# The first expert's tokens handled block by block: transposes, splits and products of 128 columns as each gather lands

## The chip, the cores and the metric

The kernel runs on one core of one Trainium2 chip. The metric is the device time of one execution in microseconds (us). Engines are called by the names of the profile: PE is TensorE (PEld its weight loads), DVE is VectorE, ACT is ScalarE, POOL is GpSimd, SP is SyncE, which issues most loads.

## The reference

Three layers stand behind one another on 3072 tokens of 512 numbers: attention with a local window and a few global keys; a mixture of 8 experts, in which each token goes to one expert and each expert takes 384 tokens; and a second feed-forward layer for all tokens. What matters here is the second layer:

```python
logits = x @ w_gate
# greedily by falling logit: each token to one expert, cap = N // E = 384 tokens each
for e in range(E):
    mask = assigned == e
    h = np.maximum(x[mask] @ w1[e], 0.0)      # 512 -> 1024
    out[mask] = h @ w2[e]                     # 1024 -> 512
# then, for all tokens: g = relu(h) + alpha * min(h, 0); g @ w_out  (512 -> 2048 -> 512)
```

## The kernel before, in words

Attention runs first and writes its rows to `x_rows` in DRAM. Then the `Router` finds the experts' token lists one expert after another, and `Experts` computes, for each expert in the order in which they are found, both feed-forward layers on its 384 tokens.

The order of instructions is written out by hand: each engine works through its own queue in the order of the program. The router is a generator, `all_phases`; each `next(gen)` issues one more piece of it between the experts' products. A phase's search is a chain of steps. One `next(gen)` issues the DVE part of a step (lines 552 to 572, then the compare of line 770, the reduce of line 778 and the preparation of line 543); the following one issues the PE product that adds the counts over the partitions (`totals`, line 786), whose result the next DVE part reads.

Numbers of the experts' layers are split in a high and a low part (types fp32r): ACT copies the high part, and another engine subtracts it to get the remainder. A product is then three: high by high, low by high, high by low (`PASSES`). For the weights (`split`, lines 887 to 892) the remainder is made by POOL; for the tokens (`x_split`) and the hidden layer (end of `up1`) by DVE.

The first expert begins as follows. When its number is known, the first tiles of its weights are loaded (`choose`). When its token list is known, `gather` issues three indirect loads on POOL, one for each block of 128 tokens. Until they land, PE computes products of no use (`filler`, line 398), each of up to 512 columns. Then `run` splits the first weight tile (line 1023), issues one DVE part of the second expert's search (line 1024), transposes all three blocks (twelve transposes into four PSUM tiles, one for each quarter of the 512 numbers), splits the four quarters, splits three more weight tiles, and calls `up1(0, 0)`: twelve products of 384 columns, four quarters by three passes. Behind them stands `next(gen)`, the `totals` product of the search, then the loop over all steps: `up1(0, 1)`, `down1(0, 0)`, and so on.

At the end of `up1` the Relu of the result is written twice, by ACT (high part, line 926) and by DVE (remainder, line 927, which waits for ACT's).

Of the kernel before, what the change touches and what calls it, by code (L numbers as in the profile page):

```python
# [9 lines left out]
FT = mybir.dt.float32  # L10
# [5 lines left out]
AF = mybir.ActivationFunctionType  # L16
OP = mybir.AluOpType
# [344 lines left out]
class Router:  # L362
# [35 lines left out]
    def filler(self, columns):  # L398
        nc = self.nc
        ps = self.spare()  # L400
        flat = self.slots.bitcast(BF).rearrange("p s t -> p (s t)")
        while columns > 0:
            n = min(columns, 512)
            nc.tensor.matmul(ps[:, :n], self.ones, flat[:, :n], start=True, stop=True)
            columns -= n
# [193 lines left out]
    def phase(self, k, result):  # L599
        nc, E, TT = self.nc, self.E, self.TT  # L600
# [25 lines left out]
        n = cnt.shape[2]  # L626
# [13 lines left out]
        if k < E - 1:  # L640
# [3 lines left out]
                                op=OP.mult)  # L644
# [15 lines left out]
        ps = self.psum.tile([128, 512], FT, name="r_ps")  # L660
# [19 lines left out]
        for name, op, s in (("r_blk", OP.logical_shift_right, B.bit_length() - 1), ("r_in", OP.bitwise_and, B - 1)):  # L680
            t = w.tile([128, TT], U16, name=name)
# [9 lines left out]
        for c in range(0, TT, chunk):  # L691
# [3 lines left out]
                                    op=OP.is_equal)  # L695
# [4 lines left out]
        ps = self.psum.tile([128, 512], FT, name="r_ps")  # L700
        yield
        for t in range(TT):
            two, one = parts[t // chunk]
            nc.tensor.matmul(ps[:rows, :B], two[:, :, t % chunk], one[:, :, t % chunk], start=(t == 0),  # L704
                             stop=(t == TT - 1))
# [8 lines left out]
        ps = self.psum.tile([128, 512], FT, name="r_ps")  # L714
        nc.tensor.matmul(ps[:, :3], lists.rearrange("p g s -> p (g s)"), self.unit, start=True, stop=True)
        if wide:
            self.filler(5120)
        yield
        idx = w.tile([128, 3], I32, name="r_idx", bufs=8)
        nc.vector.tensor_copy(idx, ps[:, :3])  # L720
# [78 lines left out]
class Experts:  # L799
# [84 lines left out]
        self.nc.sync.dma_start(r, src[:, f, :])  # L884
        self.st["r2", e, f] = r

    def split(self, name, e, f, shape):
        r = self.st.pop(("r" + name, e, f))
        s = self.pair("m_s" + name, shape, 2)
        self.nc.scalar.activation(s[:, 0], r, AF.Copy)  # L890
        self.nc.gpsimd.tensor_tensor(s[:, 1], r, s[:, 0], op=OP.subtract)  # L891
        self.st["s" + name, e, f] = s

    def split_w1(self, e, f):
# [20 lines left out]
    def up1(self, e, f):  # L915
        nc = self.nc
        s1 = self.st.pop(("s1", e, f))
        x = self.ex[e]["x"]
        n = self.NT * 128
        ps = self.hidden.tile([128, 512], FT, name="m_h", bufs=3)  # L920
        for d in range(self.ND):
            for i, (a, b) in enumerate(self.PASSES):
                nc.tensor.matmul(ps[:, :n], s1[:, a, d], x[:, b, d], start=(d == 0 and i == 0),  # L923
                                 stop=(d == self.ND - 1 and i == 2))
        h = self.pair("m_hh", [n], 2)
        nc.scalar.activation(h[:, 0], ps[:, :n], AF.Relu)  # L926
        nc.vector.scalar_tensor_tensor(h[:, 1], ps[:, :n], 0.0, h[:, 0], op0=OP.max, op1=OP.subtract)  # L927
        self.st["h", e, f] = h

    @staticmethod  # L930
    def order(n, last):
# [74 lines left out]
    def run(self, router, n_experts):  # L1006
        nf1, nf2 = self.F1 // 128, self.F2 // 128
        routes = []
        gen = router.all_phases(routes)
        while not (routes and "expert" in routes[0]):  # L1010
            next(gen)
            next(gen)
        self.choose(0, routes[0])
        while "tokens" not in routes[0]:
            next(gen)
            next(gen)
        self.gather(0, routes[0])
        nc = self.nc
        behind = self.consts.tile([1, 1], I32, name="m_behind")
        nc.gpsimd.iota(behind, pattern=[[0, 1]], base=0, channel_multiplier=0)  # L1020
        nc.sync.value_load(behind[0:1, 0:1], min_val=0, max_val=1)
        self.load_rest(0)
        self.split_w1(0, 0)
        next(gen)
        ps = [self.acc.tile([128, 512], FT, name="m_acc", bufs=4) for _ in range(self.ND)]
        for a in range(self.NT):
            for d in range(self.ND):
                self.transpose(ps[d], 0, a, d)
        for d in range(self.ND):
            self.x_split(ps[d], 0, d)  # L1030
        self.split_w1(0, 1)
        self.split_w2(0, 0)
        self.split_w2(0, 1)
        steps = [(e, s, f) for e in range(n_experts) for s, nf in ((1, nf1), (2, nf2)) for f in range(nf)]

        def prepare(e, i):
            if i == 0:
                self.split_w1(e, 0)
            elif i == 1:
                self.split_w2(e, 0)  # L1040
            elif i == 2:
                self.split_w1(e, 1)
            else:
                self.split_w2(e, 1)

        self.up1(0, 0)
        next(gen)
        self.split_w1(0, 2)
        chosen = fetched = 0
        N = len(steps)  # L1050
        for n, (e, s, f) in enumerate(steps):
            if s == 1 and f + 3 < nf1:
                self.load_w1(e, f + 3)
                self.load_w2(e, f + 3)
            full = s == 1 and f == nf1 - 1 or s == 2 and f == 0
            if not full:
                next(gen, None)
            if s == 2 and chosen == e and len(routes) > e + 1 and "expert" in routes[e + 1]:
                chosen = e + 1
                self.choose(e + 1, routes[e + 1])  # L1060
            if s == 2 and fetched == e and len(routes) > e + 1 and "tokens" in routes[e + 1]:
                fetched = e + 1
                self.gather(e + 1, routes[e + 1])
                prepared, ready = 0, n + self.READY
            now = []
            if s == 2 and e + 1 < n_experts and f >= nf2 - 6:
                while fetched > e and n >= ready and prepared < self.ND and len(now) < 1 + (f + self.ND - prepared >= nf2 or f == nf2 - 2):
                    self.x_transpose(e + 1, prepared)
                    now.append(prepared)
                    prepared += 1  # L1070
                assert f < nf2 - 2 or prepared == self.ND
            last = s == 1 and f == nf1 - 1
            ahead = self.AHEAD if e else 2
            if s == 1 and f >= nf1 - ahead:
                self.fetch_wo(e, f - nf1 + ahead)
            if e and s == 2 and f + ahead < nf2:
                self.fetch_wo(e, f + ahead)
            nx = steps[n + 1] if n + 1 < N else None
            if not last and nx:
                (self.up1 if nx[1] == 1 else self.up2)(nx[0], nx[2])  # L1080
                if nx[1] == 1 and nx[2] + 2 < nf1:
                    self.split_w1(nx[0], nx[2] + 2)
            for i in now:
                prepare(e + 1, i)
            (self.down1 if s == 1 else self.down2)(e, f, lambda: full or next(gen, None))
            if last:
                self.up2(e, 0)
            if s == 1 and f + 2 < nf1:
                self.split_w2(e, f + 2)
            if not e and s == 2 and f + 2 < nf2:  # L1090
                self.fetch_wo(e, f + 2)
# [89 lines left out]
```

## Time and profile before

| | |
|---|---|
| median of 3 runs | 1121.75 us (1120.18 to 1121.84) |
| profiled execution | 1119.95 us |
| its span in the trace | 1118.2 us |
| PE busy | 1065.7 us, 95% of the span |
| DVE, POOL, ACT busy | 68%, 48%, 34% |

The profile is that of one execution. The span runs from its first to its last instruction; the profiled execution's own time is 1.75 us longer. Times in the rows are counted from the start of the span. The granted clock of PE is a share of full speed (2.4 GHz).

### The profile page before, as it was taken

How to read it: one execution, taken by the hardware profiler on the slowest of the kernel's cores; microseconds unless marked ns; L12 is line 12 of the kernel's file. 1: busy time of each engine (PE TensorE's matmuls, PEld its weight loads, DVE VectorE, ACT ScalarE, POOL GpSimd, SP SyncE). 2: the span in 40 equal slices, each digit the busy share in tenths (PEclk: the TensorE clock that was granted, in tenths of full speed). 3: DMA queues.
4: the chain of work that ended last, by engine and by line, in shares of the span. 5: the costliest groups of instructions: out<-in, count | busy, mean ns of one | idle time of the engine just before them, and what ended most of it. 6: DMA issues, size and time to landing. Idle time of an engine off the chain costs nothing.

```text
span 1118.2 us, 19406 instructions
## 1 busy us (share of the span) xinstructions
PE 1065.7 (95%) x6659; PEld 944.2 (84%) x6659; DVE 762.9 (68%) x2228; ACT 385.6 (34%) x969; POOL 540.5 (48%) x652
## 2 busy tenths in 40 slices
PE   8989898869999999999999999999999999999997
PEld 6777677648888998899889988898899999999995
DVE  7989888778897878897789698778753323231321
ACT  7777777503322320232133113211331233123211
POOL 4888878315455823462346325432543354236222
PEclk9999999968999999999999999999999999999999
DMA  9788877114135525441534533533353435434131
GB/s 219 212 218 223 209 202 187 49 46 134 57 132 179 173 83 181 130 160 58 198 96 149 163 123 109 157 135 129 95 180 123 133 108 185 131 116 167 57 131 67
DMA packets 151219, 156.55 MB, mean 140 GB/s; under 512 B 83536, under 2 KB 116304, under 8 KB 151120
## 3 DMA queue, kind: packets, MB, share of 16 engines
q1 hardware_dynamic: 147280, 142.72, 42.3%
q0 software_dynamic: 3840, 12.59, 3.4%
q8 instruction: 53, 0.87, 0.3%
q14 instruction: 46, 0.38, 0.1%
HBM read 134.31 MB, written 20.97 MB: 139 GB/s over the span
## 4 chain that ended last, share of the span: by engine, by line
PE 75%; DVE 12%; POOL 6%; issue 3%; ACT 2%; DMA 2%; SPq 0%; DVEq 0%; POOLq 0%; ACTq 0%
PE m_h L963 23%; PE m_acc L988 23%; PE m_h L923 9%; PE m_acc L950 9%; PE a_s L212 2%; PE a_pt L232 2%; PE a_xp L248 2%; DVE r_thr L564 2%; DVE r_red L778 1%; DVE r_cmp L770 1%; PE r_ps L704 1%; POOL wo L82 1%; ACT a_p L221 1%; PE a_cb L277 1%; PE a_tp L169 1%
## 5 line engine op out<-in xcount | busy, mean ns | idle before, releaser
L973 POOL TENSOR_TENSOR m_g<-m_t,m_g 128x384 fp32r<-128x384 f32 (+1 forms) x144 | 140.2, 973 | 372.1 <-ACT m_g L972 369.1
L988 PE MATMUL m_acc<-m_so,m_g 128*128 128x512 f32 x1152 | 298.7, 399 | 0.4 <-POOL m_spacer L996 0.3
L963 PE MATMUL m_h<-m_y,wi 128*128 128x384 f32 x1536 | 294.4, 341 | 0.0
L963 PEld LDWEIGHTS m_h<-m_y,wi 128*128 128x128 f32 x1536 | 273.3, 189 | 7.5
L988 PEld LDWEIGHTS m_acc<-m_so,m_g 128*128 128x128 f32 x1152 | 209.6, 189 | 35.3 <-POOL m_g L973 0.9
L972 ACT ACTIVATE m_g<-m_t 128x384 fp32r<-128x384 f32 (+1 forms) x144 | 70.5, 490 | 435.6 <-DVE m_t L971 255.1
L891 POOL TENSOR_TENSOR m_s<-m_r,m_s 128x512 fp32r<-128x512 f32 x128 | 166.9, 1308 | 103.5 <-ACT m_s L890 103.2
L970 DVE TENSOR_SCALAR m_t<-m_h,m_al 128x384 f32<-128x384 f32 (+1 forms) x144 | 82.2, 571 | 149.2 <-PE m_h L963 136.1
L950 PE MATMUL m_acc<-m_hh,m_s 128*128 128x384 f32 x768 | 150.3, 340 | 1.3 <-DVE m_hh L927 1.3
L923 PE MATMUL m_h<-m_xt,m_s 128*128 128x384 f32 x768 | 146.1, 338 | 0.0
L923 PEld LDWEIGHTS m_h<-m_xt,m_s 128*128 128x128 f32 x768 | 136.4, 190 | 1.9 <-ACT m_xt L872 0.3
L950 PEld LDWEIGHTS m_acc<-m_hh,m_s 128*128 128x128 f32 x768 | 132.4, 188 | 2.9 <-DVE m_hh L927 1.6
L890 ACT ACTIVATE m_s<-m_r 128x512 fp32r<-128x512 f32 x128 | 79.7, 626 | 98.8 <-PE m_acc L950 34.1
L221 ACT ACTIVATE a_p<-a_sx,a_mn 128x232 f32<-128x232 f32 (+1 forms) x192 | 88.5, 462 | 25.8 <-DVE a_mn L218 25.4
L927 DVE SCALAR_TENSOR_TENSOR m_hh<-m_h,m_hh 128x384 fp32r<-128x384 f32 x64 | 35.4, 552 | 76.8 <-ACT m_hh L926 76.2
L971 DVE SCALAR_TENSOR_TENSOR m_t<-m_h,m_t 128x384 f32<-128x384 f32 (+1 forms) x144 | 73.9, 513 | 4.9
L778 DVE TENSOR_REDUCE r_red<-r_cmp 128x24 bf16<-128x576 bf16 (+1 forms) x97 | 73.9, 761 | 3.4
L218 DVE CUSTOM_DVE_ANT_0 a_sx<-a_s,a_bias 128x232 f32<-128x232 f32 (+1 forms) x192 | 61.4, 374 | 11.6 <-PE a_s L212 9.4
L212 PE MATMUL a_s<-a_kz,a_qz 64*128 64x232 f32 (+1 forms) x384 | 50.2, 381 | 18.7 <-POOL a_kz L190 16.2
L926 ACT ACTIVATE m_hh<-m_h 128x384 fp32r<-128x384 f32 x64 | 31.5, 492 | 95.6 <-PE m_h L923 82.3
L770 DVE TENSOR_TENSOR r_cmp<-r_mk,r_thr 128x576 bf16<-128x576 uint16 x78 | 61.4, 787 | 0.0
L212 PEld LDWEIGHTS a_s<-a_kz,a_qz 64*128 64x128 f32 x384 | 33.2, 193 | 28.6 <-POOL a_kz L190 22.6
(183 smaller groups left out, 1283.3 us busy)
## 6 DMA issues: line engine op xcount, KB each, us to landing
m_so<-wo_pairs SPq DMA_DIRECT2D x112, 512.0 KB, 3.3
m_r<-in_moe_w_dram SPq DMA_DIRECT2D x128, 256.0 KB, 3.0
f_raw<-in_moe_w_in_dram SPq DMA_DIRECT2D x16, 512.0 KB, 4.6
f_raw<-in_moe_w_out_dram SPq DMA_DIRECT2D x16, 512.0 KB, 3.7
wo_pairs<-m_so SPq DMA_DIRECT2D x16, 512.0 KB, 2.6
a_k<-in_k_dram SPq DMA_DIRECT2D x24, 256.0 KB, 4.8
a_q<-in_q_dram SPq DMA_DIRECT2D x24, 256.0 KB, 5.2
a_v<-in_v_dram SPq DMA_DIRECT2D x24, 256.0 KB, 4.8
```

What stands on the lines that cost most here:

```text
L212: nc.tensor.matmul(ps[s][:, a, :n], T["Q", g][r, p], kz[r, p, c0:c0 + n], start=True, stop=True)
L221: nc.scalar.activation(pr[:, s, 2 * C - n:], sx[:, s, :n], AF.Exp, bias=T["mn", g][:, h:h + 1], scale=-1.0, accum_out=T["sum", g][:, h:h + 1])
L778: nc.vector.tensor_reduce(red, cmp, axis=AX.X, op=OP.add)
L890: self.nc.scalar.activation(s[:, 0], r, AF.Copy)
L891: self.nc.gpsimd.tensor_tensor(s[:, 1], r, s[:, 0], op=OP.subtract)
L923: nc.tensor.matmul(ps[:, :n], s1[:, a, d], x[:, b, d], start=(d == 0 and i == 0), stop=(d == self.ND - 1 and i == 2))
L950: nc.tensor.matmul(ps[:, :n], s2[:, b, d * 128:(d + 1) * 128], h[:, a], start=(f == 0 and a + b == 0), stop=(last and a == 1))
L963: nc.tensor.matmul(ps[:, :n], self.wi[:, a, d, f * 128:(f + 1) * 128], y[:, b, d], start=(d == 0 and i == 0), stop=(d == self.ND - 1 and i ...
L970: nc.vector.tensor_scalar(t[:, cs], ps[:, cs], 0.0, self.al[:, f:f + 1], op0=OP.min, op1=OP.mult)
L971: nc.vector.scalar_tensor_tensor(t[:, cs], ps[:, cs], 0.0, t[:, cs], op0=OP.max, op1=OP.add)
L973: nc.gpsimd.tensor_tensor(g[:, 1, cs], t[:, cs], g[:, 0, cs], op=OP.subtract)
L988: nc.tensor.matmul(ps, g[:, a, t * 128:(t + 1) * 128], s[:, b], start=(f == 0 and a + b == 0), stop=(last and a == 1))
```

## The change

The tokens of the first expert are handled by blocks. A new function `first_up` transposes a block's four quarters into one PSUM tile, has ACT and DVE split this tile in one instruction each (512 columns), and issues twelve products of 128 columns for it; the order on PE is transposes 0, a filler, transposes 1, products 0, transposes 2, products 1, a filler, products 2. The Relu is issued at the end of `first_up`, before the splits of the next three weight tiles. The remainder of the first weight tile is made by DVE in place of POOL. The `next(gen)` that stood ahead of the transposes now stands behind the splits of the weights, directly ahead of the other one. The filler behind the last product of the token list grows from ten instructions of 512 columns to twelve.

```diff
-            self.filler(5120)
+            self.filler(6144)
...
-    def split(self, name, e, f, shape):
+    def split(self, name, e, f, shape, engine=None):
...
-        self.nc.gpsimd.tensor_tensor(s[:, 1], r, s[:, 0], op=OP.subtract)
+        (engine or self.nc.gpsimd).tensor_tensor(s[:, 1], r, s[:, 0], op=OP.subtract)
...
+        self.relu(ps, e, f)
+
+    def relu(self, ps, e, f):
+        nc, n = self.nc, self.NT * 128
...
+    def first_up(self, filler):
+        nc = self.nc
+        s1 = self.st.pop(("s1", 0, 0))
+        x = self.ex[0]["x"] = self.pair("m_xt", [self.ND, self.NT * 128], 1)
+        out = self.hidden.tile([128, 512], FT, name="m_h", bufs=3)
+
+        def part(a):
+            return slice(a * 128, (a + 1) * 128)
+
+        def turn(a):
+            ps = self.acc.tile([128, 512], FT, name="m_acc", bufs=4)
+            for d in range(self.ND):
+                nc.tensor.transpose(ps[:, part(d)], self.ex[0]["xr"][a][:, part(d)], self.ident)
+            ps = ps.rearrange("p (d t) -> p d t", t=128)
+            hi, lo = x[:, 0, :, part(a)], x[:, 1, :, part(a)]
+            nc.scalar.activation(hi, ps, AF.Copy)
+            nc.vector.tensor_tensor(lo, ps, hi, op=OP.subtract)
+
+        def multiply(a):
+            todo = [(d, i, j) for i, j in self.PASSES for d in range(self.ND)]
+            todo.sort(key=lambda m: m[2])
+            for n, (d, i, j) in enumerate(todo):
+                nc.tensor.matmul(out[:, part(a)], s1[:, i, d], x[:, j, d, part(a)], start=(n == 0),
+                                 stop=(n == len(todo) - 1))
+
+        turn(0)
+        filler(512)
+        turn(1)
+        multiply(0)
+        turn(2)
+        multiply(1)
+        filler(512)
+        multiply(2)
+        self.relu(out, 0, 0)
...
         self.load_rest(0)
-        self.split_w1(0, 0)
-        next(gen)
-        ps = [self.acc.tile([128, 512], FT, name="m_acc", bufs=4) for _ in range(self.ND)]
-        for a in range(self.NT):
-            for d in range(self.ND):
-                self.transpose(ps[d], 0, a, d)
-        for d in range(self.ND):
-            self.x_split(ps[d], 0, d)
+        self.split("1", 0, 0, [self.ND, 128], nc.vector)
+        self.first_up(router.filler)
         self.split_w1(0, 1)
         self.split_w2(0, 0)
         self.split_w2(0, 1)
...
-        self.up1(0, 0)
+        next(gen)
         next(gen)
         self.split_w1(0, 2)
```

## Rows read from the trace of the kernel before

**Rows 1.** The page: busy time, share of the span and instructions.
```profile
PE 1065.7 (95%) x6659; PEld 944.2 (84%) x6659; DVE 762.9 (68%) x2228; ACT 385.6 (34%) x969; POOL 540.5 (48%) x652
```

**Rows 2.** Waits of PE, 250 to 345 us: total us, times, longest.
```profile
PE m_acc L857 <- DMA m_x<-x_rows,r_idx: 2.5, 3, 1.0
PE m_acc L950 <- DVE m_hh L927: 1.3, 1, 1.3
```

**Rows 3.** Stretches: length, busy us of PE, PEld, DVE, ACT, POOL; granted clock; DMA.
```profile
30.00:40.00 10.00, 10.00 (x103) 8.23 (x100) 9.70 (x35) 8.55 (x27) 8.61 (x14) 1.00 0.85 233
...
242.00:246.00 4.00, 3.32 (x31) 1.94 (x29) 2.78 (x16) 0.00 (x0) 0.00 (x0) 0.93 0.23 69
246.00:248.00 2.00, 2.00 (x6) 0.78 (x7) 1.69 (x8) 0.60 (x1) 0.69 (x1) 0.50 0.78 256
...
249.00:250.00 1.00, 1.00 (x5) 0.35 (x3) 0.76 (x2) 0.00 (x0) 0.82 (x1) 0.84 0.69 147
...
252.50:253.50 1.00, 0.95 (x4) 0.56 (x4) 0.96 (x3) 0.00 (x0) 0.00 (x0) 0.62 0.76 234
...
259.00:260.00 1.00, 1.00 (x6) 0.69 (x6) 0.00 (x0) 0.35 (x1) 1.00 (x2) 0.72 0.00 0
```

**Rows 4.** Timeline, 246 to 256 us: start, us, engine, line; idle before, releaser.
```profile
246.07 3.92 PE L404 MATMUL m_h<-r_slots,r_ones 128*128 128x512 bf16 x10
...
250.75 2.03 DVE L770 TENSOR_TENSOR r_cmp<-r_mk,r_thr 128x576 bf16<-128x576 uint16 x1
...
250.91 0.66 PE L857 MATMUL m_acc<-ident,m_x 128*128 128x128 f32 x4 [0.89 <-DMA m_x<-x_rows,r_idx]
...
251.20 1.25 POOL L891 TENSOR_TENSOR m_s<-m_r,m_s 128x512 fp32r<-128x512 f32 x1
...
252.52 0.95 PE L857 MATMUL m_acc<-ident,m_x 128*128 128x128 f32 x4 [0.95 <-DMA m_x<-x_rows,r_idx]
252.81 0.75 DVE L778 TENSOR_REDUCE r_red<-r_cmp 128x24 bf16<-128x576 bf16 x1
...
254.08 1.11 PE L857 MATMUL m_acc<-ident,m_x 128*128 128x128 f32 x4 [0.61 <-DMA m_x<-x_rows,r_idx]
...
255.12 1.95 DVE L873 TENSOR_TENSOR m_xt<-m_acc,m_xt 128x384 fp32r<-128x384 f32 x4 [1.41 <-ACT m_xt L872]
...
255.14 4.48 PE L923 MATMUL m_h<-m_xt,m_s 128*128 128x384 f32 x12
```

**Rows 5.** Timeline, 259 to 264 us.
```profile
259.42 0.24 PE L786 MATMUL r_ps<-r_red,r_ones 128*128 128x24 bf16 x1
...
259.51 2.37 PE L923 MATMUL m_h<-m_xt,m_s 128*128 128x384 f32 x12
259.65 0.49 ACT L926 ACTIVATE m_hh<-m_h 128x384 fp32r<-128x384 f32 x1 [1.87 <-PE r_ps L786]
...
260.74 1.30 POOL L891 TENSOR_TENSOR m_s<-m_r,m_s 128x512 fp32r<-128x512 f32 x1 [0.15 <-ACT m_s L890]
...
261.06 1.07 DVE L564 SCALAR_TENSOR_TENSOR r_thr<-r_dig,r_pre 128x72 uint16<-128x72 f32 x1
...
262.16 0.46 DVE L770 TENSOR_TENSOR r_cmp<-r_mk,r_thr 128x576 bf16<-128x576 uint16 x1
...
262.65 0.75 DVE L778 TENSOR_REDUCE r_red<-r_cmp 128x24 bf16<-128x576 bf16 x1
...
263.46 0.19 PE L786 MATMUL r_ps<-r_red,r_ones 128*128 128x24 bf16 x1
```

**Rows 6.** Timeline, attention, 62 to 64 us.
```profile
62.88 0.66 PE L277 MATMUL a_cb<-a_cmb,a_xt 128*128 128x144 f32 x4
...
63.37 0.60 PE L169 MATMUL a_tp<-ident,a_q 128*128 128x128 f32 x4
```

**Rows 7.** Timeline of DVE, 286 to 300 us.
```profile
287.00 1.43 DVE L770 TENSOR_TENSOR r_cmp<-r_mk,r_step 128x576 bf16<-128x576 uint16 x1
...
299.59 0.23 DVE L564 SCALAR_TENSOR_TENSOR r_thr<-r_dig,r_step 128x72 uint16<-128x72 f32 x1
```

## The prediction

> **What bounds the kernel now.** I read the page first: TensorE (PE) is busy for 95% of the span [rows 1], so the question is where the other 5% lies and whether the change touches it. The waits of PE from 250 us to 345 us answer it [rows 2]: behind the three gathers of the first expert's tokens PE waits 2.5 us, and then in 90 us only 1.3 us more. Whatever delays PE's first expert therefore delays the end by as much; what shortens it shortens the end, unless a wait grows behind it. Third the table by stretches, for the clock [rows 3]: 0.93 at 242 to 246, half speed (1.2 GHz) at 246 to 248 although PE had been 83% busy before; full (2.4 GHz) within 249 to 250, during the fillers; below full again at 252.5 to 253.5, between the gathers; full again only within 259 to 260. Fourth the timeline [rows 4]: blocks of tokens arrive at 250.91, 252.52 and 254.08; the first expert's first twelve products start at 255.14 and end at 259.62, all but the last at half clock. Meanwhile VectorE (DVE) has done a search step for the second expert (its compare at 250.75 held 2.03 us, the reduce behind it). So the product with that step's sums, at 259.42, waits for nothing, and the next twelve products start at 259.51 [rows 5]. That start is my reference point: PE is full from there on.
>
> **The parts that cost nothing.** The remainder of the first weight tile leaves GpSimd (1.25 us at 251.20, [rows 4]) for DVE, right behind the search's first reduce and before the first tokens land; on DVE 512 elements cost about 0.65 us (the remainders of 384 columns, four in 1.95 [rows 4], times 4/3). It was done before the first products needed it, and will be. Three splits of 512 elements in place of four of 384 lie under PE's work on the block before. Two more fillers of 512 columns (3.92/10 = 0.39 us each at most, [rows 4]) fill time before 250.91 in which PE waits for the gather; the filler behind the first transposes lies in the next such wait. The loads queued on SP and the gathers on POOL keep their order; the next weight loads follow GpSimd's remainders, which come later, but for tiles used several steps on.
>
> **The blocks on PE.** Thirty-six products of 128 columns replace twelve of 384. The trace shows no such product in this type. Bounds: below, a third of the 384-column product at full clock, 2.37/12/3 = 0.066 us [rows 5]; above, a plain 32-bit product of 144 columns, which shows as two instructions: four for two products, 62.88 to 63.37, so 0.245 us a product [rows 6]. I take 0.122 us, the pitch of each of these four instructions, since each also brings a new 128 x 128 weight tile and the products here are one instruction each; at half clock 0.24 (the four transposes from 254.08 took 1.11 with their tail, [rows 4]). The Trainium skill, "TensorE: Matmul & The Clock Gate", section "Back-to-back issue gap", gives about 81 ns for a stream of loads and products at 128 columns; the nearest rows here show 122 [rows 6]. By the skill's figure the sum below would be an estimated 1.3 us smaller.
>
> The clock: I take it to fall after the first block as it did, because more filler and full-clock work at 242 to 246 did not keep it [rows 3], and to return at about 256.1 (steady work since 252.5; the fillers from 246.07 brought it back after 3.2 us, the products from 255.14 after about 4.3, so 255.7 to 256.9). Then: second transposes 252.52 + 4 x 0.24 = 253.48; first block, eleven products at 0.24 and one at 0.12, to 256.25; third transposes, 0.49, to 256.75; second block 12 x 0.122 = 1.46, to 258.2; filler 0.2, to 258.4; third block 1.46, to 259.9, with the tail of the last **T = 259.95**. That is no gain on 259.62: the last block is short, but the block before stands in PE's queue ahead of the last transposes.
>
> **The moved search step.** The two calls of the search now both stand behind the first expert's products. PE is in order, so the sums' product waits before the second weight tile's products, and everything behind it (the whole expert) waits too. On DVE the step stands behind the Relu remainder, which waits for the last block. [Rows 5] show this very chain once: ScalarE's Relu at 259.65, GpSimd's remainder of a weight tile at 260.74, the small multiply-add held by it (1.07 us), compare 262.16, reduce 262.65, the sums' product at 263.46: 3.81 us. Here it is longer: the splits of the second weight tile and of two others come behind the Relu, so GpSimd has its next remainder ready at once. A compare started in such a row of remainders took 1.43 us in place of 0.46 [rows 7]; about 1.1 of this falls on the chain (its start lies 0.1 into the remainder). So 0.03 + 3.81 + 1.1 + 0.1 to the next product = 5.05 us; without the second hold 3.95, without any hold (the multiply-add at 0.23 in place of 1.07 us as well, [rows 7]) 3.1. I take 5.05: next products at 265.0, **5.5 us** later than 259.51. The second tile's own remainder is ready about 2.4 us after T, so it is covered by this wait; without the wait it would cost about that, less two products.
>
> After 5 us of idle PE I expect half clock at first, as after the shorter gaps at 250 to 254 [rows 3]. Returning took 3.2 to 4.3 us of steady work, costing half of it, 1.6 to 2.2; none if the clock stays. I take **1.6**. DVE had as little waiting for it at 259.5 as it will have at 265, so nothing is given back later; the 1.3 us wait [rows 2] stays.
>
> **Sum.** 5.5 + 1.6 = +7.1. The profiled execution took 1119.95 us (span 1118.2 and 1.75 around it), so 1127.05; it lies 1.8 below the median of the runs shown (1121.75), against which I give 1121.75 + 7.1 = **1128.85**.
>
> **Rivals.**
> *Full clock kept* by the longer fillers: second transposes to 253.0, first block 254.45, third transposes 254.95, second block 256.4, filler 256.6, third 258.1, T = 258.2; + 5.05 = 263.25, + 1.6: **+5.3, 1127.1**. For it, more PE work between 249 and 252; against it, 242 to 246.
> *Half clock to the end of the blocks:* first block to 256.35, transposes 257.3, second 260.2, filler 260.6, third 263.5, T = 263.7, next 268.75: 9.2 + 1.6 = **+10.8, 1132.6**. For it, short products between weight loads; against it, the first phase, full of products of such widths [rows 6], runs at full clock at 30 to 40 us [rows 3]. The Trainium skill, same page, section "HAM oscillation — how this bites in real kernels", has short bursts between waits run at half clock each time; [rows 3] agree for the bursts between the gathers.
> *Products at the price of plain 32-bit ones, 0.245:* first block 5 cold at 0.49 and 7 at 0.245 to 257.7, transposes 258.2, second 261.1, filler 261.3, third 264.25, T = 264.4, next 269.45: 9.95 + 1.6 = **+11.5, 1133.3**. For it the row; against it, the single instruction.
> *The search wait is not there* (not slower): if the step's reduce were over before T, PE would go on at 259.95: **+0.45, 1122.2**, or -0.9 with full clock and -3 with 0.066 us products as well. It decides from a reduce that ends about 0.1 before T. Against it: DVE's order, with the Relu remainder ahead; for it: only that DVE has the time, as the step was done by 253.6 before.
>
> **How the numbers follow.** Forecast 0.41, full clock 0.20, half clock 0.10, dear products 0.10, no wait 0.19 (0.13 of it within 0.2%, 0.06 faster). 0.2%, 2.2 us, is about what a measurement tells from no change. Faster 0.06, same 0.13, slower 0.81. Forecast and full clock, with 3.1 to 5.05 of wait and 0 to 2.2 of clock, run from +1.8 to +7.7 (1123.5 to 1129.5), their own range. For 8 in 10 I reach up to the dear products, 1133.5, and down to 1122.5, just over the centre of no wait: about 0.12 left out below, 0.05 above.
>
> **What would show it.** Right: PE idle 4 to 5 us between the last block's products and the sums' product, released by DVE's reduce; compare and multiply-add of that step held near GpSimd's remainders; clock below full behind it; the products' pitch near 0.12 us at full clock; the rest of the trace shifted whole. Wrong: the sums' product within 1 us of the last block, a pitch near 0.07 or 0.24, a third block over before 257, or a stretch behind 290 us that gives time back.

## The result and the profile after

The changed kernel takes 1130.26 us in the median of six executions (1125.69 to 1132.08), the kernel before 1121.8 (1120.18 to 1122.97): ratio 1.0072, 95% interval 1.0051 to 1.0093. It is slower, by 8.5 us. Measured again, on another occasion: 1125.16 us against 1119.88, ratio 1.0053 (1.0035 to 1.0071). The profiled execution is the fastest of the first six, 1125.69 us with a span of 1124.0; against the profiled execution before that is +5.7, of which 0.8 stands ahead of the change: the first gather started that much later.

The chain is best read from the timeline, 248 to 270 us, of the changed kernel. Beside it stand [rows 4, 5].

```profile
248.11 1.21 POOL L852 DMA_INDIRECT m_x<-x_rows,r_idx  x1 [33.57 <-DVE logits L725]
...
253.70 1.53 PE L956 MATMUL m_h<-m_xt,m_s 128*128 128x128 f32 x12
...
255.07 0.63 PE L946 MATMUL m_acc<-ident,m_x 128*128 128x128 f32 x4
...
256.87 1.64 PE L956 MATMUL m_h<-m_xt,m_s 128*128 128x128 f32 x12
258.54 0.49 ACT L930 ACTIVATE m_hh<-m_h 128x384 fp32r<-128x384 f32 x1 [2.21 <-PE m_h L956]
...
259.63 5.16 POOL L891 TENSOR_TENSOR m_s<-m_r,m_s 128x512 fp32r<-128x512 f32 x4 [7.50 <-ACT m_s L890]
...
259.95 1.05 DVE L564 SCALAR_TENSOR_TENSOR r_thr<-r_dig,r_step 128x72 uint16<-128x72 f32 x1
...
261.03 1.41 DVE L770 TENSOR_TENSOR r_cmp<-r_mk,r_thr 128x576 bf16<-128x576 uint16 x1
...
262.47 0.75 DVE L778 TENSOR_REDUCE r_red<-r_cmp 128x24 bf16<-128x576 bf16 x1
...
263.29 0.20 PE L786 MATMUL r_ps<-r_red,r_ones 128*128 128x24 bf16 x1 [4.78 <-DVE r_red L778]
...
263.38 4.18 PE L923 MATMUL m_h<-m_xt,m_s 128*128 128x384 f32 x12
```

The reader is to see three things. A block's twelve products take 255.07 - 253.70 = 1.37 us, 0.114 each. The blocks are over at 258.5. And then PE stands for 4.78 us, released by the search's reduce: behind the Relu come GpSimd's four remainders in a row (5.16 us), and in that row two DVE instructions of the step are held, 1.05 and 1.41 us, where they take 0.23 [rows 7] and 0.46 [rows 5] alone; the reduce takes 0.75 here as there.

The clock of the same kernel by stretches (length, busy us of PE, granted clock, DMA share, GB/s); beside it [rows 3]:

```profile
252.00:253.00 1.00, 0.81 (x5) 1.00 0.61 213
...
257.00:258.00 1.00, 1.00 (x10) 1.00 0.72 224
...
261.00:262.00 1.00, 0.00 (x0) 0.60 0.00 0
262.00:263.00 1.00, 0.00 (x0) 0.50 0.00 0
...
267.00:268.00 1.00, 1.00 (x4) 0.50 0.24 71
268.00:269.00 1.00, 1.00 (x7) 0.98 0.00 0
```

Here the clock stays full through the gathers and blocks, falls in the wait, and the next products run at half clock until 268.

To find where time goes in each kernel, each trace is cut at three places: the start of the first gather, the start of the second twelve products of 384 columns ("second"), and that of the third twelve ("third").

| kernel | gather starts | second | third | gather to third | third to end |
|---|---|---|---|---|---|
| before | 247.31 | 259.51 | 264.11 | 16.8 | 854.1 |
| before, second trace | 248.75 | 260.77 | 265.38 | 16.6 | 852.5 |
| changed | 248.11 | 263.38 | 269.90 | 21.8 | 854.1 |
| changed, second trace | 248.33 | 265.05 | 270.70 | 22.4 | 852.3 |
| changed, third trace | 249.21 | 269.31 | 275.12 | 25.9 | 852.6 |

Behind the third twelve nothing differs beyond the spread of one kernel. All the loss beyond the spread of the gather's start lies between the gather and the third twelve: 5.0 to 9.3 us.

### The profile page after: what moved, and what is told of

Read it like the earlier page. It is cut to its first block, busy times and chain, and to the rows that moved or that the text cites. A ratio compares the mean times of both kernels' runs of the same rounds, so it can differ in the third digit from the quotient of the medians.

```text
span 1124.0 us, 19458 instructions
## 1 busy us (share of the span) xinstructions
PE 1065.8 (95%) x6685; PEld 947.0 (84%) x6687; DVE 759.3 (68%) x2228; ACT 385.5 (34%) x968; POOL 538.8 (48%) x651
## 4 chain that ended last, share of the span: by engine, by line
PE 78%; DVE 10%; POOL 6%; issue 3%; ACT 1%; DMA 1%; POOLq 0%; DVEq 0%; ACTq 0%
PE m_h L1002 23%; PE m_acc L1027 23%; PE m_acc L989 10%; PE m_h L923 10%; PE a_s L212 2%; PE a_pt L232 2%; PE a_xp L248 2%; PE a_tp L169 1%; POOL wo L82 1%; PE r_ps L704 1%; PE a_cb L277 1%; DVE r_thr L564 1%; DVE r_cmp L770 1%; DVE r_red L778 1%; POOL f_r L75 1%
## 5 line engine op out<-in xcount | busy, mean ns | idle before, releaser
L923 PE MATMUL m_h<-m_xt,m_s 128*128 128x384 f32 x756 | 143.5, 338 | 0.0
L212 PE MATMUL a_s<-a_kz,a_qz 64*128 64x232 f32 (+1 forms) x384 | 49.7, 379 | 19.9 <-POOL a_kz L190 17.4
```

The source lines that it names most:

```text
L212: nc.tensor.matmul(ps[s][:, a, :n], T["Q", g][r, p], kz[r, p, c0:c0 + n], start=True, stop=True)
```

## The experiments

The expectations were written before each run. "Wait" is that of the sums' product.

**again** and **again_2**: the changed kernel unaltered.

> The changed kernel once more, nothing altered. Its six executions so far span 1125.7 to 1132.1 us, and the profiled one is the fastest: full clock through the blocks, 4.9 us of wait for the search's sums, then half clock for about 5 us. Theory (the wait is always there, the spread is the clock): the same wait of 4.5 to 5.2 us, and, if this execution is one of the longer ones, more time at half clock in the blocks or behind them, 2 us lost for each 4 us of it. Rival (the wait itself varies): a longer execution shows a longer wait at an unchanged clock.

> The changed kernel for a third trace. The wait for the sums 4.7 to 4.9 us as in the two others; from the first gather to the second twelve products 15 to 17 us at full clock in the blocks, or 19 to 20.5 if the clock falls between the gathers (then half clock through the blocks and a time of 1128 us or more).

Measured: 1124.74 us (profiled; the six executions go from 1123.53 to 1128.75) and 1129.46 us. The wait is 4.8 us in both. The second one lost its clock just behind the wait for the second gather, which ended at 254.94: 0.82 in the stretch from 254 to 256 means half clock from about 255.3. Stretches as above, and the wait:

```profile
254.00:256.00 2.00, 1.06 (x7) 0.82 0.79 193
256.00:258.00 2.00, 2.00 (x11) 0.50 0.97 293
...
262.00:264.00 2.00, 2.00 (x11) 0.50 0.00 0
...
270.00:272.00 2.00, 2.00 (x7) 0.50 0.95 262
272.00:274.00 2.00, 2.00 (x12) 0.91 0.51 154
```

```profile
254.94 0.81 PE L946 MATMUL m_acc<-ident,m_x 128*128 128x128 f32 x4 [1.25 <-DMA m_x<-x_rows,r_idx]
...
261.42 3.02 PE L956 MATMUL m_h<-m_xt,m_s 128*128 128x128 f32 x12
...
269.22 0.20 PE L786 MATMUL r_ps<-r_red,r_ones 128*128 128x24 bf16 x1 [4.78 <-DVE r_red L778]
```

PE is busy without a gap from 256 to 264 and the clock does not return; it does at about 272.4, 3 us into the products of 384 columns that start at 269.31. Between these two executions lie 4.7 us: 3.5 from the gather to the third twelve (22.4 and 25.9), where the blocks at half clock are the difference, and 0.9 ahead of the gather. So the wait is constant in three traces and most of this spread is the clock: the rival falls. The executions above 1129.46 us have no trace.

**before_step_moved**: the kernel before, with the search step alone moved.

```diff
         self.split_w1(0, 0)
-        next(gen)
         ps = [self.acc.tile([128, 512], FT, name="m_acc", bufs=4) for _ in range(self.ND)]
...
         self.up1(0, 0)
+        next(gen)
         next(gen)
```

> The kernel before with one part of the change: the search step moved behind the first twelve products, no blocks, no new fillers, the remainder on GpSimd. Theory (the moved step is the loss): 3.1 to 4 us of wait behind the twelve products (the other splits stand ahead of the Relu here, so fewer remainders hold the step) and 1.6 to 2.2 us of half clock: +4.7 to +6.2 us, ratio 1.004 to 1.0055. Rival (the blocks are the loss): under 1 us, ratio within 1.001.

Measured: ratio 1.0051 (1.0033 to 1.0068), as for the whole change measured beside it (1.0053). Gather to third 21.7 us. The waits of PE, 245 to 350 us, of this kernel (total us, times, longest), and its timeline:

```profile
PE r_ps L786 <- DVE r_red L778: 3.8, 1, 3.8
```

```profile
263.35 1.26 POOL L891 TENSOR_TENSOR m_s<-m_r,m_s 128x512 fp32r<-128x512 f32 x1 [0.17 <-ACT m_s L890]
...
263.67 1.03 DVE L564 SCALAR_TENSOR_TENSOR r_thr<-r_dig,r_step 128x72 uint16<-128x72 f32 x1
...
264.74 0.46 DVE L770 TENSOR_TENSOR r_cmp<-r_mk,r_thr 128x576 bf16<-128x576 uint16 x1
```

The moved step alone makes a loss as large as that of the whole change. Its wait is shorter by one hold: three of the remainders stand ahead of the Relu, one behind it, and the compare is not held.

**step_before_relu**: the changed kernel, the step issued between the last block's remainder and the Relu.

```diff
-    def first_up(self, filler):
+    def first_up(self, filler, step):
...
         multiply(2)
+        step()
         self.relu(out, 0, 0)
...
-        self.first_up(router.filler)
+        self.first_up(router.filler, lambda: next(gen))
...
-        next(gen)
         next(gen)
         self.split_w1(0, 2)
```

> The search step of VectorE stands behind the last block's remainder and ahead of the Relu. Theory (the search wait sets the start of the next products): the step takes 1.9 us under the last block's products, so the sums' product goes 0.5 us after T instead of 4.9, and the next thing that PE waits for is GpSimd's remainder of the second weight tile, about 2.4 us after T, less two products: 2.5 us or more gained on the changed kernel, up to 4.5 if the clock now stays full; ratio to the kernel before 1.000 to 1.005. Rival (the weight remainder or the blocks' products set it): the next products start 4.9 us after T as now, ratio 1.007.

Measured: ratio 1.004 (1.0025 to 1.0055); its executions go from 1120.33 to 1128.12 us. The profiled one, 1120.83 us, kept full clock from 250 us on. Its timeline:

```profile
258.73 0.46 DVE L770 TENSOR_TENSOR r_cmp<-r_mk,r_thr 128x576 bf16<-128x576 uint16 x1
259.23 0.75 DVE L778 TENSOR_REDUCE r_red<-r_cmp 128x24 bf16<-128x576 bf16 x1
259.63 0.49 ACT L930 ACTIVATE m_hh<-m_h 128x384 fp32r<-128x384 f32 x1 [2.21 <-PE m_h L956]
...
260.04 0.19 PE L786 MATMUL r_ps<-r_red,r_ones 128*128 128x24 bf16 x1 [0.44 <-DVE r_red L778]
...
260.69 0.62 PE L923 MATMUL m_h<-m_xt,m_s 128*128 128x384 f32 x2 [0.47 <-ACT m_s L890]
260.72 7.80 POOL L891 TENSOR_TENSOR m_s<-m_r,m_s 128x512 fp32r<-128x512 f32 x6 [8.49 <-ACT m_s L890]
...
262.05 2.01 PE L923 MATMUL m_h<-m_xt,m_s 128*128 128x384 f32 x10 [0.74 <-POOL m_s L891]
```

The step's compare is not held and the wait falls to 0.44 us. What is late next is the second weight tile: PE waits 0.47 for its high part and, two products later, 0.74 for its remainder. Gather to third is 17.9 us, 3.9 less than in the changed kernel's first trace; in the median the gain is only 1.1 us on the changed kernel measured beside it, and the intervals of the two overlap. Executions much longer than this one remain; none of them has a trace, so what makes them long is not shown.

**splits_early**: the changed kernel with only the splits moved ahead.

```diff
         self.split("1", 0, 0, [self.ND, 128], nc.vector)
-        self.first_up(router.filler)
         self.split_w1(0, 1)
         self.split_w2(0, 0)
+        self.first_up(router.filler)
```

> The changed kernel with the splits of the second weight tile and of one tile of the second layer issued ahead of the blocks, the search step left where the change put it. Theory (the sums are what PE waits for): the remainders that hold the step are fewer, two in place of four behind the Relu, but one or two still hold it: wait of 3.8 to 4.9 us, ratio 1.003 to 1.006. Rival (GpSimd's remainder of the second weight tile is the wait): it is gone, the next products start within 1 us of the blocks' end, ratio 1.002 or less.

Measured: 1129.14 to 1130.69 us in four executions, ratio 1.0087 (1.0071 to 1.0102). Timeline:

```profile
262.20 2.49 POOL L891 TENSOR_TENSOR m_s<-m_r,m_s 128x512 fp32r<-128x512 f32 x2 [6.12 <-ACT m_s L890]
262.52 1.04 DVE L564 SCALAR_TENSOR_TENSOR r_thr<-r_dig,r_step 128x72 uint16<-128x72 f32 x1
263.59 1.41 DVE L770 TENSOR_TENSOR r_cmp<-r_mk,r_thr 128x576 bf16<-128x576 uint16 x1
...
265.84 0.20 PE L786 MATMUL r_ps<-r_red,r_ones 128*128 128x24 bf16 x1 [4.77 <-DVE r_red L778]
```

The weight tile was ready and the wait did not change: two remainders behind the Relu hold the same two instructions. So the step, not GpSimd's remainder of the second weight tile, is what PE waits for. The ratio lies above what I expected. In its trace the gather starts 1.5 us later than in the changed kernel's first and half clock lasts longer behind the wait (second to third 7.1 us instead of 6.5); why all four executions are long is not settled. This trace kept full clock through the blocks, so a time above 1129 us does not by itself tell that the blocks ran at half clock.

**step_and_splits_early**: both edits together, so that neither the step nor the tile is late.

> As step_before_relu, and the splits of the second weight tile and of one tile of the second layer are issued ahead of the blocks, so that GpSimd makes their remainders while the blocks are multiplied. Theory (the blocks themselves cost nothing, all the loss is what waits behind them): next products 0.5 us after T, no long idle stretch, clock kept when it was full; 0.5 us earlier to 1 us later than in the kernel before, ratio 0.997 to 1.001. Rival (thirty-six products of 128 columns cost more than twelve of 384 whatever stands behind): still slower, ratio 1.003 or more.

Measured: ratio 1.0023 (1.0008 to 1.0037), six of twelve executions at 1120.4 to 1121.5, one at 1122.6, five at 1124.5 to 1127.5. The profiled one (1125.61 us) belongs to the long ones and has no wait behind the blocks; its timeline and stretches:

```profile
254.33 2.80 PE L956 MATMUL m_h<-m_xt,m_s 128*128 128x128 f32 x12
...
256.93 1.07 PE L946 MATMUL m_acc<-ident,m_x 128*128 128x128 f32 x4
```

```profile
254.00:256.00 2.00, 2.00 (x12) 0.50 0.97 273
...
264.00:266.00 2.00, 2.00 (x8) 0.50 0.00 0
266.00:268.00 2.00, 2.00 (x10) 0.71 0.41 130
```

At half clock a product takes (256.93 - 254.33)/12 = 0.217 us, and over 13 us of unbroken work, from 253.57 to 267.2, pass at half speed. Neither theory is quite right: without the waits the kernel is near the one before, and the one long execution with a trace lost its clock between the gathers. That the four others did so too is likely from their times, but not shown.

**no_new_fillers**: the changed kernel with ten fillers ahead of the gather and none among the blocks.

```diff
-            self.filler(6144)
+            self.filler(5120)
...
         turn(0)
-        filler(512)
         turn(1)
...
         multiply(1)
-        filler(512)
         multiply(2)
```

> The changed kernel without its added fillers: ten ahead of the first gather, none among the blocks. Theory (short products at half clock do not bring the clock back, so without fillers it is lost between the gathers in every execution): half clock from 253 us to behind the wait, the long group of the changed kernel always, 3 to 6 us slower than its median here, ratio 1.008 to 1.010. Rival (the fillers make no difference): the ratio of the changed kernel, 1.005.

Measured: 1129.55 to 1133.6 us in four executions, ratio 1.0085 (1.0065 to 1.0105): none of the executions at 1123 to 1126 that the changed kernel has (five of twelve). Stretches:

```profile
254.00:256.00 2.00, 0.56 (x4) 0.92 0.67 208
256.00:258.00 2.00, 1.96 (x10) 0.50 0.89 260
...
274.00:276.00 2.00, 2.00 (x8) 0.50 0.09 27
```

In this trace half clock lasts from 256 to 276, the wait included. One trace proves little, but the others bear it out: in the four without the new fillers (this one, before_step_moved and the two of the kernel before) the clock falls between the arrival of the first block and that of the third; in the nine that have both the new fillers and the blocks it does so in two (again_2, step_and_splits_early). So the fillers make full clock in the blocks likely, not certain.

**remainder_on_gpsimd**: the changed kernel with the first tile's remainder back on GpSimd (`self.split("1", 0, 0, [self.ND, 128])`).

> The changed kernel with the first weight tile's remainder back on GpSimd. Theory (this part costs nothing and brings nothing): the ratio of the changed kernel within its spread, 1.004 to 1.007; the remainder ready at about 253.5 us, before the first block's weights of the low part are due. Rival (VectorE's remainder is what lets the first block start on time): the first block's products start over 0.5 us later and the end with them, 1.006 or more at the same clock.

Measured: ratio 1.0041 (1.0022 to 1.006), wait 4.8 us, gather to third 21.5: this part does nothing for the time that can be told from the spread. It shows one small thing: the third gather's instruction on POOL takes 0.95 us here, as before, and 1.08 in the changed kernel's three traces, in which DVE subtracts beside it.

**step_splits_more_fillers** and **fillers_in_both_waits**: step_and_splits_early with 1536 columns of filler behind the first transposes, and then with 1024 more between the first block's products and the third transposes.

```diff
         turn(0)
-        filler(512)
+        filler(1536)
         turn(1)
         multiply(0)
+        filler(1024)      # fillers_in_both_waits alone
         turn(2)
```

> As step_and_splits_early with 1536 columns of filler behind the first transposes in place of 512. That kernel's executions fall in two groups, 1120.4 to 1122.6 and 1124.5 to 1127.5 us, and its profiled one, of the longer group, ran the blocks and the next products at half clock from about 253.5 to 266.5 us. Theory (the groups are the clock kept or lost in the wait for the second gather): most executions now in the shorter group, median near 1121, ratio 0.9995 to 1.0015. Rival (the groups come from elsewhere, the landing of the gathers for example): the same two groups in like shares, ratio 1.002.

> step_splits_more_fillers with 1024 more columns of filler between the first block's products and the third transposes. Theory (the last executions of the longer group lose the clock in the wait for the third gather): no longer group left, median 1120 to 1121.5, ratio 0.999 to 1.001. Rival (the fillers are in the way): the third block up to 0.4 us later, ratio as before, 1.002.

Measured: 1.0018 (1.0001 to 1.0034) and 1.0014 (1.0004 to 1.0025). The profiled executions (1119.08 and 1121.88 us) keep full clock from the first transposes on, and gather to third is 17.1 and 17.4 us. The longest execution is 1127.51 in step_and_splits_early, 1127.44 and 1124.57 here, but executions of 1123.4 and more remain, four of eleven in the last kernel. So even with little late behind them the blocks are no gain on 16.6 to 16.8 us. The timeline of the first shows what stands against them:

```profile
250.70 1.08 POOL L852 DMA_INDIRECT m_x<-x_rows,r_idx  x1 [0.30 <-issue]
...
255.94 0.66 PE L946 MATMUL m_acc<-ident,m_x 128*128 128x128 f32 x4 [0.93 <-DMA m_x<-x_rows,r_idx]
...
259.85 0.19 PE L786 MATMUL r_ps<-r_red,r_ones 128*128 128x24 bf16 x1 [0.44 <-DVE r_red L778]
...
264.31 0.19 PE L786 MATMUL r_ps<-r_red,r_ones 128*128 128x24 bf16 x1 [0.52 <-DVE r_red L778]
...
264.96 2.24 PE L923 MATMUL m_h<-m_xt,m_s 128*128 128x384 f32 x12
```

From the third block's arrival to the third twelve it takes 264.96 - 255.94 = 9.0 us, two waits for the sums of 0.4 and 0.5 us included; the kernel before takes 264.11 - 254.08 = 10.0, with its first twelve products at half clock. But the third block came 5.2 us behind its instruction here and 3.95 there. These 1.3 us took the gain back; whether the change delays the landing or it was chance, no run shows.

**before_more_fillers**: the kernel before with twelve fillers and two more behind each of the first two blocks' transposes.

> The kernel before with fillers alone: twelve ahead of the first gather in place of ten, and two (1024 columns) behind the transposes of the first and of the second block; products of 384 columns, search step and splits as they were. Theory (the twelve products cost 4.5 us instead of 2.2 because the clock falls between the gathers): where the fillers hold the clock 2.2 us less, ratio 0.998 to 0.9995 over executions that hold it and some that do not; profile with 1.00 at 252 to 256 or, if it falls, as before. Rival (a filler at half clock takes 0.43 us, two 0.85, more than the 0.6 us wait, and delays the transposes): up to 0.5 us slower, ratio 1.000 to 1.0005.

Measured: ratio 1.0004 (0.9992 to 1.0017). In the trace the clock outlasts all three gathers and falls at about 258.7, behind the wait for the third, whose block comes 257.47 - 252.41 = 5.1 us behind its instruction. Below it stands the same instruction in the kernel before, 3.95 us ahead of the transposes at 254.08 [rows 4].

```profile
252.41 0.95 POOL L852 DMA_INDIRECT m_x<-x_rows,r_idx  x1 [0.31 <-issue]
...
257.47 0.66 PE L857 MATMUL m_acc<-ident,m_x 128*128 128x128 f32 x4 [1.72 <-DMA m_x<-x_rows,r_idx]
...
258.00:260.00 2.00, 1.59 (x6) 0.68 0.86 277
```

```profile
250.13 0.95 POOL L852 DMA_INDIRECT m_x<-x_rows,r_idx  x1 [0.30 <-issue]
```

The twelve products run at half clock after all. It is neither a gain nor a loss.

**before_again**: the kernel before once more.

> The kernel before once more, for a second trace. The first gather started at 247.3 us in its first trace and at 247.6 to 250.4 in the eight others, which have the same code up to there. Theory (that spread lies in the routing ahead of the change and is none of it): the start of the gather anywhere from 247 to 251, and from there to the second twelve products 12 to 14 us. Rival (the change delays the gather): 247.3 again.

Measured: 1119.58 us, the gather at 248.75, gather to third 16.6. In the traces of all kernels the gather starts between 247.3 and 250.4 us: that spread lies ahead of the change.

No run beat the kernel before.

## Why the prediction was right, and where it was not

The forecast was +7.1 us, 1128.85; measured were +8.5 (1130.26) and, the second time, +5.3. The direction and the cause were right, one step of the path was not.

**The moved search step** is the main loss, as forecast. Forecast for its wait: 5.05 us to the next products; measured 263.38 - 258.54 + 0.03 = 4.87, with both holds where they were put: the multiply-add 1.05 (forecast 1.07), the compare 1.41 (1.43). The rival that the wait is not there fell in all seven traces that have the step behind the Relu: 3.8 to 4.8 us.

**The half clock behind the wait**, forecast 1.6 us: second to third is 6.52 us in the changed kernel and 4.60 before, so 1.9, within the bounds 1.6 to 2.2. In the two other traces it is 5.65 and 5.81, so 1.0 and 1.2, below them: there the clock came back 2.8 and 3.0 us into the products, here after 4.7.

**The products of 128 columns**, forecast 0.122 us at full clock and 0.24 at half: measured 0.114 and 0.217. The lower bound (0.066) and the upper (0.245) were both far off. The Trainium skill's figure for such a stream ("TensorE: Matmul & The Clock Gate", section "Back-to-back issue gap", 81 ns) is 29% below what the trace has for these 32-bit weights.

**The clock between the gathers** is the step that failed. My likeliest case had it fall after the first block and return at 256.1, in the middle of the blocks. No trace shows that. It either stays full to the end of the blocks, with the total that I gave for that rival (forecast +5.3; +5.7 in the profiled execution, +4.8 for 1124.74), or it falls and does not return before the products of 384 columns (forecast for that rival +10.8; measured 1129.46 - 1119.95 = +9.5). The forecast of +7.1 lies between the two, and a median came out near it: that is luck, as no traced execution went the way that gave it. How many of the untraced executions were of which kind is not shown. I had let the clock return on products of 128 columns as it had on fillers of 512 [rows 4]; in again_2 they ran 9 us without a gap at half clock. The Trainium skill, same page, section "HAM oscillation — how this bites in real kernels", which stood beside that rival, has short bursts between waits run at half clock. again_2 agrees in so far as its blocks run at half clock behind a wait of 1.25 us; that they stay there through 9 us without a wait is not what the section describes.

**The parts that cost nothing.** The remainder on DVE: confirmed within the spread. The fillers cost nothing in the waits, also confirmed, but I had given them a value in a rival alone, and the traces with and without them (no_new_fillers) make it likely that the blocks run at full clock because of them.

**That nothing is given back later** held: third to end is 852.3 to 854.6 us in all fourteen traces.

**Two slips in the working** that change nothing of this: the view behind [rows 2] has a third wait in the 90 us, 0.7 us for the router (PE r_ps L704), which the changed kernel has too; and "-0.9 with full clock", without the wait, comes to 258.2 - 259.51 = -1.3.

## What to carry to other kernels

Before moving a piece of work later in a hand-written order, look at what its consumer stands in front of: this step was free where its engine idled, and cost 4.8 us of the busiest engine behind a Relu. When several instructions of GpSimd become ready together, look which of VectorE's are held beside them (here the multiply-add and the compare, not the reduce), and issue the step that somebody waits for ahead of them. Cutting a product into narrower ones cost PE time here: three products of 128 columns take 0.34 us at full clock where one of 384 takes 0.20, and in some executions all 36 ran at half clock. How much of the first is the weight tile loaded for each product, no run took apart.

## What the runs showed of the hardware

In again_2 the granted clock stayed at half from 255.3 to 272.4 us: through 9 us of PE busy without a gap on the blocks (products of 128 columns, transposes and one filler), through the wait, and for the first 3 us of the products of 384 columns. step_and_splits_early and no_new_fillers show over 9 us of such blocks at half clock as well. In the changed kernel's three traces the clock came back 2.8 to 4.7 us into the products of 384 columns, 4.4 and 4.8 us into them in the two of the kernel before. What makes the difference no run took apart.

Beside a remainder of GpSimd, VectorE's multiply-add took 1.03 to 1.07 us in the rows shown, in place of 0.23, and its compare 1.41 to 1.43 in place of 0.46; the reduce behind them took 0.75 in either case.

A gather of 128 rows landed between 3.6 us (kernel before, first block, 247.31 to 250.91) and 5.6 us (again, third block, 251.14 to 256.71) after its instruction on POOL, a spread wider than any single wait that the fillers were to fill (up to 1.7 us).
